# Seventh group's scores on strips, filler shared out, no single score ahead of strips

## The chip, the cores and the metric

The kernel runs on one core of a Trainium2 chip. The time is the device time of one execution in microseconds; the figure quoted is the median over runs. The engines are the PE (TensorE, matrix products), ScalarE (ACT), VectorE (DVE), GpSimd (POOL) and SP, which mainly issues DMA transfers.

## The reference

Two independent parts share one launch, and their outputs are put side by side.

```python
def _A_ref(x, wq, wk, wv, wo):          # x [1, 2048, 448], 16 heads of 28
    q = (x @ wq) as [heads, 2048, 28]
    k = x @ wk ; v = x @ wv             # one key/value head for all
    p = softmax(q @ k.T * 28 ** -0.5)
    return concat_heads(p @ v) @ wo

def _B_ref(x, w_r, w_i):                # x [1, 2048, 448]
    return irfft2(rfft2(x) * (w_r + 1j * w_i), s=(2048, 448))
```

All tensors are float32.

## The kernel before, in words

The kernel opens with the projections, the key tables and the first stage of the Fourier transform (the first 70 us or so). The rest, which the change concerns, is one long loop over the attention.

**Groups, chunks and steps.** The 2048 queries are cut into four chunks of 512, the 16 heads into four sets of four. A *group* is one chunk with one set, 16 groups in all, numbered 0 to 15 in the code; the text also says "seventh group" for number 6. A group has 16 *steps*, one for each 128 keys, so there are 256 steps. A step computes the scores of four heads against 128 keys (four products of 512 columns), ScalarE takes their exponentials out of the PSUM banks into `p`, and the PE multiplies them with the values (`values`, line 1218), summing a group's 16 steps in bank 7. The other seven banks serve scores and filler.

**Two ways to compute scores.** To keep float32 accuracy, keys and queries are split into a high and a low part, and a score is the sum of three products: high by high, high by low, low by high.

- A *stacked* step (`score`, line 1146) has the parts stacked over the 128 rows of the PE: `ka` holds the keys, `qa` the queries of a group. Each head's score is one product. `qa` is put together from `qh` and `ql` by nine DMAs of SP (lines 218, 219).
- A *strip* step (`strips`, line 1169) uses the PE as four strips of 32 rows, one for each head, at once. Each score takes three products, so a step has 12: four of high keys by high queries, four of high keys by low queries, four of low keys by high queries. It needs the keys repeated on all four strips. At the start these copies are in `kh` and `kl`. `STRIPS` (line 36) lists the groups that work on strips.

**Where the later strips' keys are kept.** `kh` and `kl` share their two buffers with the normed attention outputs, which are called `oh` (high part) and `ol` (low part), one pair for each chunk. From group 4 on those buffers belong to the outputs. So a later group on strips needs a fresh copy: `copy_keys` (line 787) writes the keys over the `oh` and `ol` of a chunk whose output projection is finished, in four DMAs of 512 KB from `ka` on SP's queue, two for `oh` (partitions 0 to 63 and 64 to 127) and two for `ol`. `KEYS` (line 38) says which copy each group takes. In the traces, products that read such a copy are named by `oh` and `ol`.

**What follows a group.** `group_out` copies bank 7 to `qraw`, and four rows of sums take a way through DRAM: out, back in another shape (`rs`), reciprocal on VectorE (`group_sums`, line 1038), out, and back spread over the partitions (`R`). `group_norm` (line 1049) multiplies and splits into `oh` and `ol`. When a chunk's four groups are normed, the chunk's four *output units* (`w_unit`) become ready. Each is the output projection of 128 rows: 11 products at line 1071, in pieces of 2, 3, 3 and 3. `wo_out` (line 1075) copies the result to `ya` and SP stores it. After the fourth unit of a chunk `copy_keys` follows.

**Filler.** Output units and the units of the last Fourier stage (`z_unit`, line 973, and `y_unit`, line 999) are *filler*: the PE does them between the scores of stacked steps. Strip steps take none. The middle of the Fourier part is VectorE's background work on the tile `X`, put between the other things that VectorE does; its result goes through DRAM (line 932) to the `z` units (loads at line 963).

**What sets the order.** Python code writes every engine's order out when the program is built. A loop keeps a clock for each engine (`clk`), a time at which each bank comes free (`free`), and a heap of events (`after`) with planned times; it decides step by step whether the PE takes scores, values or filler. `size` chooses how many steps' values are taken together (four where filler is at hand, else two), `share` how much filler a block may take. These planned times only decide the order; on the chip, the engines wait for each other through semaphores.

Of the kernel before, what the change touches and what calls it, by code (L numbers as in the profile page):

```python
# [32 lines left out]
LEAD = 7  # L33
WARM = 8, 8
FIRST = 8
STRIPS = 0, 1, 2, 3, 4, 7, 12, 15
HOME = {1: 0, 3: 1, 4: 0, 7: 1, 12: 0, 15: 1}
KEYS = {7: 0, 12: 1, 15: 2}
PLACES = (3, 5, 6, 8, 9, 10)


# [57 lines left out]
def kernel(ctx: ExitStack, tc: tile.TileContext, t: dict):  # L99
# [124 lines left out]
    with tc.tile_pool(name="f1", bufs=2) as f1[0], tc.tile_pool(name="w1", bufs=1) as w1, ExitStack() as ctx1:  # L224
# [305 lines left out]
        for c in range(1, NC):  # L530
            for g in range(NG):
                n = 4 * (c - 1) + g
# [152 lines left out]
    def after(when, dur, f, *a):  # L685
        heapq.heappush(events, (when, next(serial), dur, f, a))
# [339 lines left out]
    def group_out(c, g):  # L1026
        o = osb[c, g] = qraw[:, g, c * CW:c * CW + CW]
        V.tensor_copy(o, bank[7])  # L1028
        taken_out[0] += 1
        sd = dp.tile([4, CW], F32, name="sd", bufs=2)  # L1030
        rd = dp.tile([4, CW], F32, name="rd", bufs=2)
        rs = ap.tile([128, 16], F32, name="rs")
        nc.gpsimd.dma_start(sd, o[DH::32])  # L1033
        nc.gpsimd.dma_start(rs, sd.rearrange("i (a b) -> (i a) b", b=16))
        after(clk["dve"] + 10.0, 0.3, group_sums, c, g, rs, rd)

    def group_sums(c, g, rs, rd):
        V.reciprocal(rs, rs)
        nc.gpsimd.dma_start(rd.rearrange("i (a b) -> (i a) b", b=16), rs)
        for i in range(4):  # L1040
            nc.gpsimd.dma_start(R[32 * i:32 * i + DH], rd[i:i + 1].to_broadcast([DH, CW]))  # L1041
        after(clk["dve"] + 12.0, 2.1, group_norm, c, g)

    def group_norm(c, g):
        if g == 0:
# [227 lines left out]

    total = 12 * 2.22 + 16 * (0.88 + 0.73)

    def share(n):
        return max(1.8, n * (total - done[0]) / max(234 - done_steps, 3)) if n > 2 else 0.0

    done_steps, quota = 0, 0.0
    sc = 0  # L1280
    while done_steps < 256:
        k = sc // 4
        if 4 * k == sc and k // 16 in STRIPS and k < 256 and (done_steps >= k - 2 or not k):
            assert not waiting and KEYS.get(k // 16, -1) in spread_keys
            if k:
                vector(clk["pe"])
            strips(k)
            sc += 4
            if k < 2:
                first_fill(L + k)  # L1290
            while done_steps <= k - 2:
                values(done_steps, 1)
                done_steps += 1
                exps()
            n, since, gap, quota = size(), 0, 2, 0.0
            continue
# [3 lines left out]
        t_v = end[need - 1]  # L1300
        soon = min(free) <= clk["pe"] + 0.05
        more = sc < 4 * limit()
        if t_v <= clk["pe"] + 0.05 and (sc >= min(need + LEAD, 4 * limit()) or not soon):
            values(done_steps, n)
            done_steps += n
            exps()
            n = size()
            since, gap, quota = 0, 2, share(n)
        elif can_fill() and quota > 0 and since >= EARLY and gap >= 2 and (cur[0] or soon):
            t0 = done[0]  # L1310
            fill()
            quota -= done[0] - t0
            gap = 0
        elif more and soon:
            score(sc)
            sc += 1
            since += 1
            gap += 1
        elif sc == 1024 and can_fill():
            fill()  # L1320
        elif sc == 1024 and parts and normed[NC - 1] == NG - 1 and t_v > clk["pe"] + 0.5:
            partial()
        elif t_v <= min(free) or not more:
            values(done_steps, n)
            done_steps += n
            exps()
            n = size()
            since, gap, quota = 0, 2, share(n)
        else:
            score(sc)  # L1330
            sc += 1
            since += 1
            gap += 1
# [150 lines left out]
```

## Time and profile before

| | |
|---|---|
| median of 3 runs | 625.97 us (625.66 to 625.98) |
| profiled execution, span from first to last instruction | 624.6 us |
| what lies around the span (625.97 - 624.6) | 1.4 us |
| PE busy / ACT busy / DVE busy / POOL busy | 99% / 87% / 55% / 15% of the span |
| mean granted PE clock | 1.000 |
| DMA, mean over the span | 105 GB/s, 65.31 MB |

The busy times are shares of the whole span and so mix stages with different limits. A row of the timeline holds the start, the duration, the engine, the line, the tiles and the count of instructions merged into it; a bracket at its end tells how long the engine idled before it and who ended that. The records of the PE overlap, because its products are pipelined, so the pace is read from one row's start to the next row's start and not from durations. A row of the windows view gives, for a stretch of time, its length and then the busy time of PE, PEld, DVE, ACT and POOL with the count of instructions, the granted clock, the share of the 16 DMA engines and GB/s. The values of one step appear as eight records in the trace (each product runs in two passes) and as four rows in the program's order.

### The profile page before, as it was taken

The page shows a single profiled execution, that of the slowest core. Times are in us where ns is not written, and L with a number is a line of the kernel's source. Part 1 is how long each engine was busy: PE and PEld are TensorE (multiplying, and loading weights), DVE is VectorE, ACT ScalarE, POOL GpSimd, SP SyncE. Part 2 cuts the span into 40 slices and gives each one's busy share as a digit, 9 for nine tenths or more (in the row PEclk, how much of TensorE's full clock was granted, in tenths as well). Part 3 has the DMA queues.
Part 4 walks back from the last instruction along what each step waited for, and adds up shares of the span by engine and source line. Part 5 has one row for each costly group of instructions (what it writes and reads, how often), then busy time and mean ns, then how long its engine had stood idle before and what let it go on. Part 6 is the DMA issues. An engine that isn't in the chain of part 4 may idle for free.

```text
span 624.6 us, 13634 instructions
## 1 busy us (share of the span) xinstructions
PE 619.0 (99%) x5367; PEld 319.4 (51%) x5367; DVE 344.1 (55%) x685; ACT 541.0 (87%) x977; POOL 90.7 (15%) x168
## 2 busy tenths in 40 slices
PE   9999999999999999999999999999999999999997
PEld 7877633333333346654345565656653346564335
DVE  6999604979698987897732513227451231321014
ACT  4645799999999998889999888878889998888993
POOL 1021130102121101020321210030210101020200
PEclk9999999999999999999999999999999999999999
DMA  8856794001123331171664242294213131016001
GB/s 304 276 134 171 193 247 185 16 20 46 34 90 88 87 76 47 40 161 28 211 213 104 77 119 78 61 215 147 82 60 94 34 98 34 16 66 149 18 1 59
DMA packets 28748, 65.31 MB, mean 105 GB/s; under 512 B 6514, under 2 KB 15826, under 8 KB 27270
## 3 DMA queue, kind: packets, MB, share of 16 engines
q1 hardware_dynamic: 21066, 43.25, 24.9%
q0 software_dynamic: 7472, 20.96, 11.3%
q8 instruction: 42, 0.69, 0.5%
q10 hardware_dynamic: 144, 0.23, 0.1%
q14 instruction: 24, 0.19, 0.1%
HBM read 30.35 MB, written 16.30 MB: 75 GB/s over the span
## 4 chain that ended last, share of the span: by engine, by line
PE 98%; ACT 1%; DMA 1%; DVE 0%; issue 0%; DVEq 0%; ACTq 0%
PE banks L1218 39%; PE banks L1146 21%; PE banks L1169 18%; PE banks L330 7%; PE banks L1071 6%; PE banks L973 2%; PE banks L161 2%; PE banks L999 2%; PE banks L171 1%; DMA raw<-xw 1%; ACT p L1185 0%; PE banks L592 0%; DVE bs L188 0%; PE banks L502 0%; ACT al L615 0%
## 5 line engine op out<-in xcount | busy, mean ns | idle before, releaser
L1203 ACT ACTIVATE p<-banks 128x512 f32<-128x512 f32 x512 | 256.5, 702 | 39.4 <-PE banks L1218 18.3
L1218 PE MATMUL banks<-p,vs 128*32 128x512 f32 x2048 | 254.5, 600 | 0.2 <-DVE bs L188 0.2
L1185 ACT ACTIVATE p<-banks 128x512 f32<-128x512 f32 x262 | 145.5, 614 | 1.5 <-PE banks L1169 1.2
L1146 PE MATMUL banks<-qa,ka 128*128 128x512 f32 x512 | 145.7, 407 | 0.0
L1183 ACT ACTIVATE p<-banks 128x1024 f32<-128x1024 f32 x125 | 129.3, 1034 | 0.0
L1146 PEld LDWEIGHTS banks<-qa,ka 128*128 128x128 f32 x512 | 90.6, 188 | 53.3 <-ACT p L1203 34.5
L1218 PEld LDWEIGHTS banks<-p,vs 128*32 128x32 f32 x2048 | 49.3, 108 | 112.4 <-issue 108.7
L1028 DVE COPY qraw<-banks 128x512 f32<-128x512 f32 x15 | 10.4, 691 | 68.6 <-PE banks L1218 68.6
L1033 POOL DMA_DIRECT2D sd<-qraw x15 | 8.9, 596 | 244.1 <-DVE qraw L1028 244.1
L1075 DVE COPY ya<-banks 128x448 f32<-128x448 f32 x12 | 7.5, 624 | 52.2 <-PE banks L1071 36.4
L1041 POOL DMA_DIRECT2D R<-rd x60 | 30.4, 513 | 39.4 <-DMA rd<-rs 36.5
L1169 PE MATMUL banks<-qa,oh 32*128 32x512 f32 x384 | 35.6, 443 | 0.0
L1169 PE MATMUL banks<-qa,kh 32*128 32x512 f32 x384 | 35.5, 443 | 0.0
L856 DVE SCALAR_TENSOR_TENSOR X<-w,X 128x226 f32<-128x226 f32 (+2 forms) x72 | 34.1, 473 | 2.4
L1169 PEld LDWEIGHTS banks<-qa,kh 32*128 32x128 f32 x384 | 14.5, 183 | 40.3 <-ACT p L1185 40.3
L1169 PEld LDWEIGHTS banks<-qa,oh 32*128 32x128 f32 x384 | 14.6, 183 | 38.5 <-ACT p L1185 37.7
L981 DVE CAST zh<-banks 113x512 fp32r<-113x512 f32 (+1 forms) x16 | 11.0, 685 | 27.9 <-ACT p L1203 27.0
L1005 DVE COPY w<-banks 128x256 f32<-128x256 f32 x16 | 6.8, 423 | 35.0 <-PE banks L999 31.9
L334 ACT ACTIVATE qraw<-banks 128x512 f32<-128x512 f32 x16 | 9.4, 599 | 17.8 <-PE banks L330 17.7
L330 PE MATMUL banks<-xh,wqh 128*128 128x512 f32 x64 | 24.3, 412 | 0.2 <-DVE xh L278 0.2
L1071 PE MATMUL banks<-woh,oh 128*128 128x448 f32 x64 | 23.6, 369 | 0.0
L1071 PE MATMUL banks<-wol,oh 128*128 128x448 f32 x64 | 23.1, 362 | 0.0
(139 smaller groups left out, 754.6 us busy)
## 6 DMA issues: line engine op xcount, KB each, us to landing
xb<-xb SPq DMA_DIRECT2D x8, 512.0 KB
qa<-qa SPq DMA_DIRECT2D x8, 512.0 KB
ob<-yo SPq DMA_DIRECT2D x16, 256.0 KB
X<-t POOLq DMA_DIRECT2D x8, 452.0 KB, 15.5
wf<-w POOLq DMA_DIRECT2D x8, 452.0 KB, 3.9
c<-t POOLq DMA_DIRECT2D x8, 452.0 KB, 4.4
R<-rd POOLq DMA_DIRECT2D x60, 56.0 KB, 2.4
t<-bs SPq DMA_DIRECT2D x14, 226.0 KB
```

The lines of the kernel that those rows point to most:

```text
L161: mm(pa[r0:r0 + 32, e, 113 * k:113 * k + 113], f[:, 2 * r + k, 2 * p + e, h], cs1[:, 2 * r + k], start=True, stop=True)
L330: mm(pq[c, g], w[:, j, gs], x[:, j], start=(j == 0 and n == 0), stop=(j == 3 and n == 1))
L856: todo(226 * n, lambda d=d, q=q: STT(both(d), t[0].rearrange("p r n f -> p r (n f)"), q, both(a), op0=ALU.mult, op1=ALU.add))
L973: mm(pz[:w, j], fb["c2", q % 2][:, e, j, :w], fb["fi", q % 2][:, j], start=True, stop=True)
L1041: nc.gpsimd.dma_start(R[32 * i:32 * i + DH], rd[i:i + 1].to_broadcast([DH, CW]))
L1071: mm(p, x[c][:, g, s], w[:, m], start=(g == 0 and n == 0), stop=(g == NG - 1 and n == 2))
L1146: mm(bank[b], ka[:, kc * 128:(kc + 1) * 128], qa[c, g][:, h], start=True, stop=True)
L1169: mm(bank[bs[i]], k[r, kc * 128:(kc + 1) * 128], q[r], start=(n == 0), stop=(n == 2))
L1183: nc.scalar.activation(ends[1], banks[:, bs[1]:bs[1] + 2], AF.Exp, scale=SCALE)
L1185: nc.scalar.activation(pt[4 * st + i], bank[bs[i]], AF.Exp, scale=SCALE)
L1203: nc.scalar.activation(p, bank[b], AF.Exp, scale=SCALE)
L1218: mm(bank[7][32 * i:32 * i + 32], vs[:, kc], pt.pop(4 * st + i), start=(kc == 0), stop=(kc == 15))
```

## The change

Five things differ:

- Group 6 joins `STRIPS`; its keys are copy 0, the one that group 7 already uses.
- `group_sums` and `group_norm` are planned 3 us earlier each.
- `share` works toward two goals: by step 92 the first chunk's four output units are done (9.0 us of planned filler), by step 237 all filler. What is left is divided among the stacked steps alone.
- Filler pieces may stand one score apart (before: two) while much filler is left in a block.
- The last score of a stacked group is taken ahead of the values (`last`), so that it does not stand alone ahead of the strips.

```diff
-STRIPS = 0, 1, 2, 3, 4, 7, 12, 15
+STRIPS = 0, 1, 2, 3, 4, 6, 7, 12, 15
-KEYS = {7: 0, 12: 1, 15: 2}
+KEYS = {6: 0, 7: 0, 12: 1, 15: 2}
...
-        after(clk["dve"] + 10.0, 0.3, group_sums, c, g, rs, rd)
+        after(clk["dve"] + 7.0, 0.3, group_sums, c, g, rs, rd)
...
-        after(clk["dve"] + 12.0, 2.1, group_norm, c, g)
+        after(clk["dve"] + 9.0, 2.1, group_norm, c, g)
...
+    goals = (92, 9.0), (237, total)
+
     def share(n):
-        return max(1.8, n * (total - done[0]) / max(234 - done_steps, 3)) if n > 2 else 0.0
+        until, goal = next((x for x in goals if x[0] > done_steps + 2), goals[-1])
+        left = sum(st // 16 not in STRIPS for st in range(done_steps, until))
+        return n * (goal - done[0]) / max(left, 3) if n > 2 else 0.0
...
         if 4 * k == sc and k // 16 in STRIPS and k < 256 and (done_steps >= k - 2 or not k):
-            assert not waiting and KEYS.get(k // 16, -1) in spread_keys
             if k:
                 vector(clk["pe"])
+            assert not waiting and KEYS.get(k // 16, -1) in spread_keys
             strips(k)
...
         more = sc < 4 * limit()
-        if t_v <= clk["pe"] + 0.05 and (sc >= min(need + LEAD, 4 * limit()) or not soon):
+        last = more and sc == 4 * limit() - 1 and min(free) <= clk["pe"] + 0.35
+        if t_v <= clk["pe"] + 0.05 and (sc >= min(need + LEAD, 4 * limit()) or not soon) and not last:
             values(done_steps, n)
...
-        elif can_fill() and quota > 0 and since >= EARLY and gap >= 2 and (cur[0] or soon):
+        elif can_fill() and quota > 0 and since >= EARLY and gap >= (2 if quota < 2.3 else 1) and (cur[0] or soon):
...
-        elif more and soon:
+        elif more and (soon or last):
             score(sc)
```

The order of the instructions shows where this lands. The PE, where the kernel before goes from the stacked steps of group 6 to the strips of group 7 (values at `p,vs`, stacked scores at `qa,ka`, strip products at `qa,oh` and `qa,ol`; the brackets name the semaphores that a row waits for, those with DMAHW being landings of SP's transfers):

```order
L1146 MATMUL banks<-qa_1057,ka 128x512 [waits Activation_49] x8
L1218 MATMUL banks<-p,vs 32x512 x8
L1146 MATMUL banks<-qa_1057,ka 128x512 [waits Activation_49]
L1169 MATMUL banks<-qa_1058,oh 128x512 [waits DMAHW2_49,Activation_49]
L1169 MATMUL banks<-qa_1058,oh 128x512
L1169 MATMUL banks<-qa_1058,oh 128x512 [waits DMAHW3_49,Activation_49]
L1169 MATMUL banks<-qa_1058,oh 128x512 [waits Activation_49]
L1169 MATMUL banks<-qa_1058,oh 128x512 x4
L1169 MATMUL banks<-qa_1058,ol 128x512 [waits DMAHW4_49]
L1169 MATMUL banks<-qa_1058,ol 128x512
L1169 MATMUL banks<-qa_1058,ol 128x512 [waits DMAHW5_49]
```

Ahead of the strips stands a single score, and between it and the block with the first chunk's last output unit five pairs of stacked steps. The PE in the changed kernel, at its first product on a copied key, now in group 6:

```order
L1071 MATMUL banks<-woh,ol 128x448
L1146 MATMUL banks<-qa_1058,ka 128x512 [waits Activation_49] x5
L1218 MATMUL banks<-p,vs 32x512 x16
L1169 MATMUL banks<-qh,oh 128x512 [waits DMAHW1_49,DVE_49]
L1169 MATMUL banks<-qh,oh 128x512 [waits Activation_49]
L1169 MATMUL banks<-qh,oh 128x512 [waits DMAHW2_49,Activation_49]
L1169 MATMUL banks<-qh,oh 128x512 [waits Activation_49]
L1169 MATMUL banks<-ql,oh 128x512 x4
L1169 MATMUL banks<-qh,ol 128x512 [waits DMAHW3_49]
L1169 MATMUL banks<-qh,ol 128x512
L1169 MATMUL banks<-qh,ol 128x512 [waits DMAHW4_49]
L1169 MATMUL banks<-qh,ol 128x512
```

The single score is gone, and between the last product of the first chunk's output units (`woh,ol`) and the first strip product stand five scores and the values of four steps. SP's queue, as the difference between the two kernels, around the copy that these strips read:

```order
-L218 DMA qa_1057<-qh 32x512
-L218 DMA qa_1057<-ql 32x512
-L219 DMA qa_1057<-qa_1057 64x2048
 L1077 DMA oa<-ya 128x448 x2
 L1057 DMA lows<-ol 128x512
```

The nine transfers that build the stacked queries of group 6 are gone; the copy itself (line 793, four transfers) stands in the same place behind the fourth store of `ya`.

## The prediction

> **What bounds the kernel now.** I read the page's chain of waits first, then the timeline of the PE in the stretches that the change rewrites, then the DMA queue.
>
> ```profile
> PE 98%; ACT 1%; DMA 1%; DVE 0%; issue 0%; DVEq 0%; ACTq 0%
> ```
>
> The chain that ends last runs on the PE for 98% of the span, so a microsecond counts if it is put into the PE's order or taken out of it. Three kinds of steps share that order. A stacked pair without filler, around 280 us:
>
> ```profile
> 275.73 2.14 PE L1146 MATMUL banks<-qa,ka 128*128 128x512 f32 x8
> 277.80 1.93 PE L1218 MATMUL banks<-p,vs 128*32 128x512 f32 x16
> 279.65 2.11 PE L1146 MATMUL banks<-qa,ka 128*128 128x512 f32 x8
> 281.69 1.92 PE L1218 MATMUL banks<-p,vs 128*32 128x512 f32 x16
> 283.54 2.14 PE L1146 MATMUL banks<-qa,ka 128*128 128x512 f32 x8
> ```
>
> The first column is the start. Two steps (eight scores, then the values of two steps) take 279.65 - 275.73 = 3.92 us, the next pair 3.89, and no row carries a bracket for an idle PE. A strip step, and how strips are entered:
>
> ```profile
> 291.37 0.50 PE L1146 MATMUL banks<-qa,ka 128*128 128x512 f32 x1
> 291.80 0.74 PE L1169 MATMUL banks<-qa,oh 32*128 32x512 f32 x8
> 292.36 0.41 PE L1169 MATMUL banks<-qa,ol 32*128 32x512 f32 x4
> ...
> 296.50 1.06 PE L1218 MATMUL banks<-p,vs 128*32 128x512 f32 x8
> ...
> 298.40 1.06 PE L1218 MATMUL banks<-p,vs 128*32 128x512 f32 x8
> ```
>
> One strip step takes 298.40 - 296.50 = 1.90 us. The single score ahead of the strips takes 0.43 us (291.37 to 291.80). Within a strip step the third product, the only one that reads the low keys `ol`, starts 0.56 us after the first. Last, a block of four stacked steps with a whole output unit as filler:
>
> ```profile
> 261.97 1.66 PE L1146 MATMUL banks<-qa,ka 128*128 128x512 f32 x6
> 263.47 0.36 PE L1071 MATMUL banks<-woh,oh 128*128 128x448 f32 x1
> ...
> 266.83 0.36 PE L1071 MATMUL banks<-woh,ol 128*128 128x448 f32 x1
> 267.03 1.08 PE L1146 MATMUL banks<-qa,ka 128*128 128x512 f32 x4
> 268.04 3.64 PE L1218 MATMUL banks<-p,vs 128*32 128x512 f32 x32
> 271.61 2.34 PE L1146 MATMUL banks<-qa,ka 128*128 128x512 f32 x9
> ```
>
> This is the last output unit of the first chunk. Its last product starts at 266.83. Call T = 267.03 the start of the score behind it. Then come 1.01 us for four scores (so 0.25 for one), and 3.57 us for the values of four steps.
>
> **The change part by part.** *The seventh group on strips.* By the order, the stacked pairs fall from 17 to 9, the blocks of four stay at 23, and 16 steps become strip steps. Eight pairs of about 3.905 us leave (31.24), 16 strips of 1.90 come (30.40): -0.84. The eight `qa` copies and the big ninth one for this group leave SP's queue; nothing on the PE waited for them.
>
> *No lone head.* Three entries into strips lose their single score, which then stands in a block: 0.43 - 0.23 = 0.20 each, -0.60 together. I take 0.23 from the pair (1.85 us of scores and a little over 0.2 of switching make 2.07).
>
> *Filler shared out.* The number of filler products stays the same and the PE is the bound with and without them, so moving them costs and gains nothing: 0. One place bounds a gain:
>
> ```profile
> 510.22 2.04 PE L1146 MATMUL banks<-qa,ka 128*128 128x512 f32 x6
> 512.10 1.03 PE L973 MATMUL banks<-fi,c 128*113 128x128 f32 x8
> ```
>
> Six scores between two filler pieces last 1.88 us where the six at 261.97 last 1.50. That stall may go (-0.4) or come up elsewhere (+0.4). I keep 0, as most fillers show none.
>
> *Sums and norms placed earlier.* The vector engine may now stand longer at a landing.
>
> ```profile
> L1049 DVE TENSOR_TENSOR qraw<-qraw,R 128x512 f32<-128x512 f32 x15 | 10.3, 685 | 13.7 <-DMA R<-rd 13.7
> L1038 DVE RECIPROCAL rs<-rs 128x16 f32<-128x16 f32 x15 | 3.7, 247 | 10.2 <-DMA rs<-sd 10.1
> ```
>
> It waits 24 us in 30 such places already, with no term of it on the chain. Up to 3 us more each would have to push a bank's eviction or the first filter outputs, which are loaded well ahead of the PE:
>
> ```profile
> 320.38 0.71 POOL L963 DMA_DIRECT2D c<-t  x1
> ...
> 335.28 1.03 PE L973 MATMUL banks<-fi,c 128*113 128x128 f32 x8
> ```
>
> The load is issued 15 us before its product. I take 0, between 0 and +2 if that cover is used up.
>
> *The keys for the seventh group.* This is the term that decides. `KEYS` gives group 6 the copy 0 of the keys, which overwrites `oh` and `ol` of the first chunk. So it cannot start before the first chunk's last output unit has read them, and strips of group 6 cannot start before it has landed. Before, this copy served group 7:
>
> ```profile
> 267.94 0.33 SPq L1077 DMA_DIRECT2D oa<-ya  x1
> 268.31 1.13 SPq L793 DMA_DIRECT2D oh<-ka  x2
> 269.55 4.49 SPq L793 DMA_DIRECT2D ol<-ka  x2
> ```
>
> ```profile
> 268.00:269.00 1.00, 1.00 (x13) 0.37 (x16) 1.00 (x4) 0.49 (x2) 0.00 (x0) 1.00 0.21 81
> ...
> 278.00:279.00 1.00, 1.00 (x12) 0.26 (x8) 0.97 (x4) 1.00 (x4) 0.52 (x1) 1.00 0.89 197
> 279.00:280.00 1.00, 1.00 (x10) 0.31 (x3) 1.00 (x5) 1.00 (x4) 1.00 (x3) 1.00 0.26 90
> ```
>
> The last two columns are the DMA engines' share and GB/s. The four copies of 512 KB are issued from T + 1.28 on, and the transfers keep the engines full until 279.6 or so, T + 12.6: together with the 224 KB of `ya` some 2.3 MB at about 200 GB/s. Strips of group 7 came at 291.80, 12 us later, so nobody waited.
>
> After the change the last unit sits in the last stacked block before the strips. Behind T stand only five scores and four steps of values: 1.01 + 0.23 + 3.57 = 4.81 us. The first strip product is reached at T + 4.81, its third at T + 5.37. The high keys arrive half by half and end about midway through the copy, the second half of the low keys at T + 12.6. The wait is 12.6 - 5.4 = **7.2 us**, cut in pieces by the products whose half has landed. Behind it on the PE's queue stands everything; ScalarE has no scores to exponentiate, the vector engine's copy of the sixth group's output waits for values behind the strips, and its filter work waits behind that copy, late by the same time as the PE that will use it. No work is placed in the gap. Afterwards a strip step costs 1.90 as before, so nothing is made up.
>
> Bounds of the wait: the two other copies are the nearest rows.
>
> ```profile
> 406.80 1.66 SPq L793 DMA_DIRECT2D oh<-ka  x2
> ...
> 420.00:422.00 2.00, 2.00 (x13) 1.55 (x10) 0.00 (x0) 1.61 (x4) 0.00 (x0) 1.00 0.96 239
> ...
> 562.68 1.13 SPq L793 DMA_DIRECT2D oh<-ka  x2
> ...
> 572.00:574.00 2.00, 2.00 (x18) 0.44 (x17) 0.00 (x0) 2.00 (x5) 0.00 (x0) 1.00 0.72 160
> ```
>
> The third took until about 573.5, 10.8 us from its issue, which makes the wait 6.7; the second ran into other loads and lasted about 14 us, which makes it 9.9. Nothing else large is due at this place (the store of the filter work starts some 40 us later), so I take 7.2.
>
> The sum: -0.84 - 0.60 + 7.2 = +5.8 us. The profiled span of 624.6 becomes 630.4; the runs' median lies 1.37 above the span (625.97), so **631.7 us**.
>
> [...]
>
> **The rivals.**
>
> *A: the PE's clock falls as well.* Inside the program the PE has not stood still for microseconds; at its two ends it has:
>
> ```profile
> 1.07 3.59 PE L253 MATMUL banks<-idle 128*128 128x256 bf16 x16 [1.07 <-DVE warm L248]
> ...
> 5.16 1.77 PE L330 MATMUL banks<-xh,wqh 128*128 128x512 f32 x4 [0.17 <-DVE xh L278]
> 6.76 0.62 PE L330 MATMUL banks<-xl,wqh 128*128 128x512 f32 x2
> ```
>
> ```profile
> 620.39 0.37 PE L1071 MATMUL banks<-woh,ol 128*128 128x448 f32 x1
> ...
> 624.00:624.60 0.60, 0.00 (x0) 0.00 (x0) 0.00 (x0) 0.00 (x0) 0.00 (x0) 0.73 0.00 0
> ```
>
> At the start four products of 512 columns take 6.76 - 5.16 = 1.60 us, later ones 0.23 each: the PE ran slow until about 6.5, 5.4 us after its first product. At the end the granted clock of the last 0.6 us averages 0.73, so it halved at about 624.3, 3.5 us after the last product. For this rival: the wait of 7.2 us is twice that. Against: it is cut by products at the landings, into pieces of under 3 us each (the high keys' two halves, then the low keys' two, some 2.5 us apart), and the rows do not show whether such short bursts keep the clock up. Price: half speed for up to 5.4 us loses up to 2.7 us: 631.7 + 2.7 = 634.4. [...] Chance 0.25.
>
> *B: the copy lands later still*, because another transfer shares the engines or `ya` reaches SP late: the second copy's 14 us, wait 9.9 in place of 7.2: 634.4. For it: one of three copies was so. Against: at 406 filter loads ran beside it, which at 256 to 269 are not due yet. Chance 0.10.
>
> *C: faster.* The copy lands before the strips ask for it, and 1.44 us are won: 624.5. It needs the low keys by T + 5.4, so 2.3 MB in the 4.1 us behind the issue: 560 GB/s. The stretch with the most traffic had 410:
>
> ```profile
> 10.00:12.00 2.00, 2.00 (x11) 1.65 (x10) 1.71 (x3) 1.01 (x3) 0.00 (x0) 1.00 1.03 410
> ```
>
> So it would need a first strip that asks for less than the whole copy; but the first strip step reads all four partition groups of both key tiles. Chance 0.05. *D: in between,* the copy runs near that 410 GB/s: 5.7 us, landing at T + 7.0, wait 1.6, total +0.2: 626.1, no change. Chance 0.05.
>
> **How the numbers follow.** Forecast 0.55, A 0.25, B 0.10, C 0.05, D 0.05. The forecast's own range, from a wait of 6.7 with the stall at 510 gone (-0.4) to one of 7.5 with 0.7 of delays on the vector engine, is 630.8 to 632.7. The range for 8 in 10 takes in A and B to a little over their 634.4 and leaves out C and D: 630.5 to 635.5. A measurement of this kernel tells some 0.2% (1.25 us) from no change: faster is C (0.05), the same is D with a remainder below it (0.04), slower is the rest (0.91).
>
> **What would show it.** Right: one stretch in the changed kernel, between the sixth group's last stacked block and its first strip values, in which the PE's products of the high and low keys (`oh`, `ol`) stand singly with idle brackets that name the copy, 6.5 to 8 us in all; the copy's issue 1.3 us behind the last output product of the first chunk; strip steps at 1.90 us before and after; stacked blocks at 9.6 to 11 us by the number of their filler products; the three entries into strips directly behind the values; no wait at the entries of groups 12 and 15, where 19 us and more lie between the last output unit and the strips. A is right if the first strips behind the gap take more than 1.90 each and the granted clock of that stretch is under 1. Wrong: no gap at that place (then C, and the time is near 624.5), or a gap and yet a time under 630, which would mean that the shared filler won something that I priced at 0. A second gap, at the first filter products of the ninth group, would mean that the vector engine's earlier waits did cost.

## The result, and the profile after

The changed kernel takes 635.76 us (median, 635.23 to 636.11), the kernel before 625.93 on the same chip: a ratio of 1.0158, 95% interval 1.0143 to 1.0172, so about 9.8 us slower. The forecast was 631.7 with a range up to 635.5: the sign and the place were right, the size was not, and rival A (the clock) came true, though its own 634.4 was 1.4 us short as well.

The profiled execution has a span of 634.0 us against 624.6, so 9.4 more. First the view of the windows, three stages of the loop in the kernel before and then in the changed one: from the first stacked block behind group 4's strips to the block with the ninth group's first filter products, from there to the end of group 12's strips, and from there to the end of the loop.

```profile
221.67:333.79 112.12, 112.12 (x824) 54.31 (x820) 79.77 (x179) 105.50 (x201) 16.97 (x30) 1.00 0.40 113
333.79:504.34 170.55, 170.55 (x1256) 95.95 (x1252) 64.08 (x122) 147.41 (x284) 25.16 (x45) 1.00 0.35 95
504.34:608.70 104.36, 104.36 (x787) 53.09 (x783) 20.95 (x39) 94.51 (x177) 11.19 (x21) 1.00 0.22 57
```

```profile
220.85:342.90 122.05, 115.88 (x952) 50.81 (x948) 80.42 (x181) 104.65 (x187) 17.50 (x31) 0.96 0.33 95
342.90:512.97 170.07, 170.07 (x1250) 95.25 (x1246) 63.20 (x118) 147.19 (x282) 24.60 (x44) 1.00 0.34 94
512.97:618.04 105.07, 105.07 (x792) 53.77 (x788) 22.20 (x42) 94.58 (x177) 11.19 (x21) 1.00 0.21 57
```

All of the loss is in the first stage: 122.05 - 112.12 = +9.93. The second stage has -0.48, the third +0.71. Only the first stage of the changed kernel has an idle PE (122.05 - 115.88 = 6.17 us) and a clock under 1. What comes ahead of these stages is 0.82 shorter, which has nothing to do with the change: in this execution the first four products at line 330 took 1.01 us, where they took 1.60 in the kernel before, and the lead of 0.8 is there before 70 us.

The PE's timeline of the changed kernel at the sixth group's end, the place that the prediction named:

```profile
254.84 0.36 PE L1071 MATMUL banks<-woh,ol 128*128 128x448 f32 x1
255.04 1.53 PE L1146 MATMUL banks<-qa,ka 128*128 128x512 f32 x5
256.51 3.64 PE L1218 MATMUL banks<-p,vs 128*32 128x512 f32 x32
261.06 0.50 PE L1169 MATMUL banks<-qh,oh 32*128 32x512 f32 x2 [0.92 <-DMA oh<-ka]
263.76 0.49 PE L1169 MATMUL banks<-qh,oh 32*128 32x512 f32 x2 [2.20 <-DMA oh<-ka]
263.77 0.81 PE L1169 MATMUL banks<-ql,oh 32*128 32x512 f32 x4
266.13 0.80 PE L1169 MATMUL banks<-qh,ol 32*128 32x512 f32 x2 [1.55 <-DMA ol<-ka]
268.43 0.79 PE L1169 MATMUL banks<-qh,ol 32*128 32x512 f32 x2 [1.50 <-DMA ol<-ka]
269.15 1.94 PE L1218 MATMUL banks<-p,vs 128*32 128x512 f32 x8
271.01 0.80 PE L1169 MATMUL banks<-qh,oh 32*128 32x512 f32 x4
...
274.46 0.51 PE L1169 MATMUL banks<-qh,oh 32*128 32x512 f32 x4
```

T, the start of the score behind the last output product, is 255.04. Without a wait the strips would begin 3.57 us behind the values, at 260.08, and their third product at 260.64. The four brackets are the landings of the four halves of the keys; the last lands at 268.43 = T + 13.39, so the **wait is 268.43 - 260.64 = 7.8 us**. Two strip steps later, at 274.46, the PE should have been at 260.08 + 2 x 1.90 = 263.88. It lost 10.58 in all, so **2.8 us besides the wait**, and the values of one step, which take 1.07 at full speed, take 1.94. The view of the windows of that stretch:

```profile
260.00:262.00 2.00, 0.65 (x6) 0.21 (x2) 1.97 (x5) 0.71 (x2) 0.00 (x0) 1.00 0.95 197
262.00:264.00 2.00, 0.23 (x4) 0.27 (x6) 1.81 (x5) 0.00 (x0) 0.00 (x0) 1.00 0.98 229
264.00:266.00 2.00, 0.58 (x6) 0.06 (x2) 0.31 (x1) 0.00 (x0) 0.00 (x0) 0.57 1.01 221
266.00:268.00 2.00, 0.80 (x2) 0.29 (x2) 0.00 (x0) 0.99 (x2) 0.00 (x0) 0.50 0.57 139
...
272.00:274.00 2.00, 2.00 (x16) 0.20 (x8) 0.00 (x0) 1.25 (x3) 0.00 (x0) 0.50 0.00 0
274.00:276.00 2.00, 2.00 (x24) 0.65 (x20) 1.40 (x3) 1.28 (x3) 0.42 (x1) 0.87 0.00 0
```

The granted clock is 0.5 from (1.00 - 0.57) x 2 / 0.5 = 1.72 us ahead of 266.00 to (1.00 - 0.87) x 2 / 0.5 = 0.52 us behind 274.00: 264.28 to 274.52, 10.24 us. It fell while the wait still lasted and stayed low for 6 us after the last key had landed. Of the four executions on record two have a mean granted clock of 0.991, as the profiled one, and two 0.995, and these two were no faster (636.11 and 635.68 us against 635.84 and 635.23); how their loss divides into wait and clock no trace tells. The DMA engines are full at some 200 to 230 GB/s until 267. SP's queue in the changed kernel, to be read beside its rows at 268 in the kernel before:

```profile
246.81 9.47 SPq L1077 DMA_DIRECT2D oa<-ya  x2
256.39 1.19 SPq L793 DMA_DIRECT2D oh<-ka  x2
257.67 4.47 SPq L793 DMA_DIRECT2D ol<-ka  x2
```

The copy is issued at T + 1.35 (before: T + 1.28).

### The profile page after: what moved, and what is told of

Its sections match the earlier page's. It is cut to its first block, busy times and chain, and to the rows that moved or that the text cites. A ratio compares the mean times of both kernels' runs of the same rounds, so it can differ in the third digit from the quotient of the medians.

```text
span 634.0 us, 13892 instructions
## 1 busy us (share of the span) xinstructions
PE 622.3 (98%) x5495; PEld 315.3 (50%) x5495; DVE 344.7 (54%) x685; ACT 540.0 (85%) x963; POOL 90.7 (14%) x168
## 4 chain that ended last, share of the span: by engine, by line
PE 97%; DMA 1%; ACT 1%; SPq 0%; DVE 0%; issue 0%; DVEq 0%; ACTq 0%
PE banks L1218 38%; PE banks L1169 20%; PE banks L1146 18%; PE banks L330 7%; PE banks L1071 6%; PE banks L973 2%; PE banks L161 2%; PE banks L999 2%; DMA ol<-ka 1%; PE banks L171 1%; PE banks L253 1%; ACT p L1185 0%; SPq L793 0%; PE banks L592 0%; DVE bs L188 0%
## 5 line engine op out<-in xcount | busy, mean ns | idle before, releaser
L1218 PE MATMUL banks<-p,vs 128*32 128x512 f32 x2048 | 257.9, 604 | 0.2 <-DVE bs L188 0.2
L1203 ACT ACTIVATE p<-banks 128x512 f32<-128x512 f32 x448 | 224.5, 666 | 39.3 <-PE banks L1218 21.0
L1185 ACT ACTIVATE p<-banks 128x512 f32<-128x512 f32 x298 | 165.1, 614 | 12.8 <-PE banks L1169 6.4
L1183 ACT ACTIVATE p<-banks 128x1024 f32<-128x1024 f32 x139 | 143.8, 1035 | 0.0
L1146 PE MATMUL banks<-qa,ka 128*128 128x512 f32 x448 | 129.0, 407 | 0.0
L1146 PEld LDWEIGHTS banks<-qa,ka 128*128 128x128 f32 x448 | 79.0, 188 | 43.0 <-ACT p L1203 26.7
L1049 DVE TENSOR_TENSOR qraw<-qraw,R 128x512 f32<-128x512 f32 x15 | 10.3, 688 | 27.0 <-DMA R<-rd 26.9
```

Of the source, the lines that this page charges most:

```text
L1146: mm(bank[b], ka[:, kc * 128:(kc + 1) * 128], qa[c, g][:, h], start=True, stop=True)
L1183: nc.scalar.activation(ends[1], banks[:, bs[1]:bs[1] + 2], AF.Exp, scale=SCALE)
L1185: nc.scalar.activation(pt[4 * st + i], bank[bs[i]], AF.Exp, scale=SCALE)
L1203: nc.scalar.activation(p, bank[b], AF.Exp, scale=SCALE)
L1218: mm(bank[7][32 * i:32 * i + 32], vs[:, kc], pt.pop(4 * st + i), start=(kc == 0), stop=(kc == 15))
```

## The experiments

"Lost in the gap" below is worked out as above: the third strip step's start, less the place where it would be without a wait.

**1. The group taken off strips again.** Everything else of the change stays; the first goal becomes 10.0 so that the copy comes in time for group 7.

```diff
-STRIPS = 0, 1, 2, 3, 4, 6, 7, 12, 15
-KEYS = {6: 0, 7: 0, 12: 1, 15: 2}
+STRIPS = 0, 1, 2, 3, 4, 7, 12, 15
+KEYS = {7: 0, 12: 1, 15: 2}
...
-    goals = (92, 9.0), (237, total)
+    goals = (92, 10.0), (237, total)
```

> The change without its first part: the seventh group stays on stacked scores (the first goal of the filler is raised from 9.0 to 10.0, so that the first chunk's last piece still fits ahead of the copy). Theory (the wait for the copied keys and the slow clock behind it are the whole loss of 10 us): no wait anywhere, granted clock 1.00 throughout, and the time of the kernel before less what the three lone scores cost (0.6) plus what single blocks lose to ScalarE (up to 1): 625.3 to 626.5. Rival (the spread filler, the earlier sums and norms or the kept-back last score carry part of the loss): 628 or more.

Measured 627.25, ratio 1.0022 (1.0013 to 1.0032), mean granted clock 0.999: between the two ranges. The copied keys cost the main part, but the rest of the change (here with the first goal at 10.0), for which the prediction has a gain of 0.6, costs 1.2 to 1.4 (by the medians and by the ratio). Experiments 5 and 6 follow this.

**2. The gap filled.** The wait stays, but the PE works through it: 33 products without use ahead of group 6's first strip.

```diff
     def strips(st):
...
+        if st == 96:
+            for _ in range(33):
+                mm(bank[bs[0]], ka[:, :128], ka[:, 512:1024], start=True, stop=True)
```

> The changed kernel with 33 extra products of 512 columns ahead of the first strip product of the seventh group, about 7.6 us of work at 0.23 each, into a bank that the strips then overwrite; the PE is busy while the copy lands. Theory (the clock is a cost of its own, 2.8 us by the strips behind the gap, and it falls because the PE stands nearly still): the copy lands as before, the clock stays at 1.00 and the time falls by 2.5 to 3.0, to about 633. Rival (the slow stretch is only another sign of the wait, or products do not hold the clock): 635.5 to 636.

Measured 633.48, ratio 1.0118 (1.0101 to 1.0135). The PE's timeline, with the dummies and the one wait that is left:

```profile
255.74 1.53 PE L1146 MATMUL banks<-qa,ka 128*128 128x512 f32 x5
257.20 3.64 PE L1221 MATMUL banks<-p,vs 128*32 128x512 f32 x32
260.78 7.78 PE L1168 MATMUL banks<-ka 128*128 128x512 f32 x33
268.49 0.50 PE L1172 MATMUL banks<-qh,oh 32*128 32x512 f32 x4
...
270.01 0.50 PE L1172 MATMUL banks<-qh,ol 32*128 32x512 f32 x2 [0.56 <-DMA ol<-ka]
```

The copy landed at T + 14.27, 0.9 later than in the changed kernel, and still the first stage, now 221.54 to 341.77, is 122.05 - 120.23 = 1.8 us shorter; the mean granted clock is 0.999 in place of 0.991. So the clock's fall is a cost of its own, set by the idle PE and not by the copy, and 1.8 + 0.9 = 2.7 agrees with the 2.8 worked out above. By the medians of four runs each the kernel is 2.3 us faster.

**3. The output units earlier.** All four stand in the first two stacked blocks of the sixth group's stretch, and the copy starts 6 us sooner.

```diff
-    goals = (92, 9.0), (237, total)
+    goals = (89, 9.0), (237, total)
```

> The changed kernel with the first goal at step 89 in place of 92: the first chunk's four output units stand in two blocks instead of three, so that 12.2 us of other work lie between the last unit and the first strip. Theory (only the distance to the copy's landing counts, some 12.6 to 13 us behind the last unit): a wait of under 0.5 us at the third strip product, clock 1.00, time 625.3 to 626.5. Rival (strips in the seventh group cost something beside the wait, or the copy moves back with the units' denser filler): 628 or more.

Measured 626.35, ratio 1.0007 (0.9996 to 1.0018). SP's queue and the PE at the first strip:

```profile
250.09 1.19 SPq L793 DMA_DIRECT2D oh<-ka  x2
```

```profile
260.89 0.51 PE L1169 MATMUL banks<-qh,oh 32*128 32x512 f32 x4
261.22 0.40 PE L1169 MATMUL banks<-ql,oh 32*128 32x512 f32 x4
261.45 0.39 PE L1169 MATMUL banks<-qh,ol 32*128 32x512 f32 x2
262.03 0.50 PE L1169 MATMUL banks<-qh,ol 32*128 32x512 f32 x2 [0.18 <-DMA ol<-ka]
```

One wait of 0.18 is left and the clock stays up (mean 0.999), with the same strips, the same copy and the same source. For the gap, only the distance between the last output unit and the first strip counts. No gain over the kernel before remains, though: the three stages differ from its by +0.12, -0.66 and +0.71 us, so the third loses what the second wins (experiments 5 and 6).

**4. What sets the copy's rate.** The prediction took 200 GB/s from the rows without knowing what makes it. Three variants: the keys written to DRAM early and read from there onto 64 partitions at a time; the same, onto all 128 at once; and the two halves from `ka` on two queues.

```diff
+    kd = dp.tile([2, 64, S], F32, name="kd")     # filled early from kh and kl
...
-                nc.sync.dma_start(d[64 * u:64 * u + 64].bitcast(F32), ka[64 * k:64 * k + 64].bitcast(F32))
+                nc.sync.dma_start(d[64 * u:64 * u + 64].bitcast(F32), kd[k])
```

> The changed kernel with the keys written to DRAM once, early (2 transfers of 512 KB behind the first key tables), and every later copy read from there instead of from the stacked keys in SBUF. Theory (the copy is slow because both its ends lie in SBUF: 200 GB/s in each of the four copies traced, where loads from DRAM ran at up to 410): the copy is through some 6 us after its issue, the wait shrinks to 2 to 3 us, the clock stays at 1.00, time 626.5 to 628. Rival (SP's queue or the size of the pieces sets 200 GB/s): the copy takes 10 to 11 us as before, 635 to 636.

```diff
+    kd = dp.tile([2, 128, S], F32, name="kd")
...
-            for u in range(2):
-                nc.sync.dma_start(d[64 * u:64 * u + 64].bitcast(F32), ka[64 * k:64 * k + 64].bitcast(F32))
+            nc.sync.dma_start(d.bitcast(F32), kd[k])
```

> The changed kernel, with the keys of all heads written to DRAM early (two of 1 MB) and each copied key tile read from there by one transfer of 1 MB onto all 128 partitions, where the change sends two transfers of 0.5 MB onto 64 partitions each. Theory: a transfer onto 64 partitions reaches half of what one onto 128 does, and that sets the 180 to 229 GB/s in the stage of the copy. Then the two copies land some 5 us sooner after their issue, the third product waits 2 to 3 us in place of 7.8, the clock stays nearly full and the time is 626.5 to 628.5. Rival: what sets the rate is something else (the queue, the size of its packets): the copies take the same 10 us, the wait stays at 7 to 8 us, the clock falls and the time is 635 to 637.

```diff
-                nc.sync.dma_start(d[64 * u:64 * u + 64].bitcast(F32), ka[64 * k:64 * k + 64].bitcast(F32))
+                (nc.gpsimd if u else nc.sync).dma_start(d[64 * u:64 * u + 64].bitcast(F32), ka[64 * k:64 * k + 64].bitcast(F32))
```

> The changed kernel with the two halves of each copied key tile issued from two queues, SyncE's and GpSimd's, so that both can run at once; the source stays SBUF. Theory that one queue works off its transfers one after another and each alone runs at about 200 GB/s: the copies land 4 to 5 us sooner, the wait is 2 to 4 us, the time 626.5 to 629. Rival, that the sixteen DMA engines or the ports of SBUF set the rate whichever queue issues: the copies take the same 10 us, the time is 635 to 637.

Measured: 637.07 (ratio 1.0179, 1.0162 to 1.0196) from DRAM in halves, 631.41 (1.0080, 1.0064 to 1.0095) from DRAM onto all partitions, 634.21 (1.0123, 1.0107 to 1.0138) on two queues. None of the three lies in a range that was named. The last landings in the PE's timeline, first in halves from DRAM, then onto all partitions, then on two queues:

```profile
266.38 0.79 PE L1174 MATMUL banks<-qh,ol 32*128 32x512 f32 x2 [1.07 <-DMA ol<-kd]
268.67 0.79 PE L1174 MATMUL banks<-qh,ol 32*128 32x512 f32 x2 [1.50 <-DMA ol<-kd]
```

```profile
257.52 3.64 PE L1222 MATMUL banks<-p,vs 128*32 128x512 f32 x32
263.39 0.50 PE L1173 MATMUL banks<-qh,oh 32*128 32x512 f32 x4 [2.23 <-DMA oh<-kd]
265.74 0.50 PE L1173 MATMUL banks<-qh,ol 32*128 32x512 f32 x4 [1.62 <-DMA ol<-kd]
...
270.60 0.50 PE L1173 MATMUL banks<-qh,oh 32*128 32x512 f32 x4
```

```profile
266.80 0.92 PE L1169 MATMUL banks<-qh,oh 32*128 32x512 f32 x4 [5.69 <-DMA oh<-ka]
```

In halves, the last 512 KB land 2.3 us behind those ahead of them, whether from DRAM (268.67 - 266.38 = 2.29) or from SBUF (268.43 - 266.13 = 2.30): 228 GB/s. Onto all partitions, the second 1 MB lands 265.74 - 263.39 = 2.35 us behind the first: 446 GB/s. The fullest window of 2 us has 229 GB/s in both runs in halves, and 418 in the one onto all partitions. The source made no difference; the number of partitions written did, by a factor of two. The transfer onto all partitions was also twice as large, but the size does not set the rate: at the start of the kernel before four transfers of 512 KB onto all 128 partitions (`raw`, line 267) stand on the queue with only 40 KB beside them, and the DMA engines moved 410 GB/s between 4.00 and 6.00 us. The last low key now lands 9.7 us behind T (256.06 there), not 13.4, and 5.7 us are lost in the gap (270.60 less 257.52 + 3.57 + 3.80), not 10.6. My expectation of 626.5 to 628.5 still missed: the first of the two transfers took 6.0 us from its issue (257.40) to its landing, and the clock fell to half for 3.4 us (the last section shows it). On two queues all four halves are there 10.8 us behind T, with one wait of 5.69 us ahead of them, so two queues overlap a part, with at most 311 GB/s in a window of 2 us.

Why a transfer onto 64 partitions goes at half the rate, none of these runs shows.

**5. The small parts one by one,** each put alone into the kernel before: the last score kept back (no lone heads); the shared filler; the earlier sums and norms.

```diff
-        if t_v <= clk["pe"] + 0.05 and (sc >= min(need + LEAD, 4 * limit()) or not soon):
+        last = more and sc == 4 * limit() - 1 and min(free) <= clk["pe"] + 0.35
+        if t_v <= clk["pe"] + 0.05 and (sc >= min(need + LEAD, 4 * limit()) or not soon) and not last:
...
-        elif more and soon:
+        elif more and (soon or last):
```

> The kernel before with one part of the change alone: the last score before a strips step is kept back until two or more stand together (no lone head). By the prediction's term this is worth -0.60 us (three lone scores of 0.20): 625.4. By what the two traces and the run with group 6 stacked showed since: the score that is kept back arrives in a longer run of scores, and these runs wait for ScalarE to free a bank (nine scores in a row cost 2.97 in place of 2.33); then the gain is eaten up and the kernel takes 626.0 to 627.2.

```diff
+    goals = (92, 10.0), (237, total)
+
     def share(n):
-        return max(1.8, n * (total - done[0]) / max(234 - done_steps, 3)) if n > 2 else 0.0
+        until, goal = next((x for x in goals if x[0] > done_steps + 2), goals[-1])
+        left = sum(st // 16 not in STRIPS for st in range(done_steps, until))
+        return n * (goal - done[0]) / max(left, 3) if n > 2 else 0.0
...
-        elif can_fill() and quota > 0 and since >= EARLY and gap >= 2 and (cur[0] or soon):
+        elif can_fill() and quota > 0 and since >= EARLY and gap >= (2 if quota < 2.3 else 1) and (cur[0] or soon):
```

> The kernel before with the shared filler alone (the new share and the shorter gap), first goal 10.0 so that its keys of group 7 come as early as before. By the prediction's term (0, bounds -0.4 and +0.4) it takes 625.6 to 626.4. By what the run with group 6 stacked showed (+1.2 with share, early sums and no lone heads together, and no lone heads alone within 0.6 of nothing) the share costs it: 627.0 to 627.7, in waits of scores for banks that ScalarE frees.

```diff
-        after(clk["dve"] + 10.0, 0.3, group_sums, c, g, rs, rd)
+        after(clk["dve"] + 7.0, 0.3, group_sums, c, g, rs, rd)
...
-        after(clk["dve"] + 12.0, 2.1, group_norm, c, g)
+        after(clk["dve"] + 9.0, 2.1, group_norm, c, g)
```

> The kernel before with the earlier sums and norms alone (7.0 and 9.0 in place of 10.0 and 12.0 in the planner). By the prediction's term (0, bound +2) it takes 625.6 to 626.4: the planner's units come one stacked pair earlier, and their number stays. Rival: this is where the run with group 6 stacked lost its 1.2, by units that fall into blocks with too little between their scores: 627.0 or more.

| alone in the kernel before | median us | ratio, 95% interval | first stage | second | third |
|---|---|---|---|---|---|
| no lone heads | 625.80 | 0.9993 (0.9984 to 1.0002) | +0.02 | +0.09 | -0.25 |
| shared filler | 627.56 | 1.0024 (1.0015 to 1.0033) | +0.63 | -0.37 | +1.32 |
| earlier sums and norms | 626.40 | 1.0006 (0.9997 to 1.0015) | -0.09 | -0.19 | +0.27 |
| group 6 stacked (experiment 1) | 627.25 | 1.0022 (1.0013 to 1.0032) | +0.54 | -0.51 | +0.80 |

The last columns are the length of the three stages less that of the kernel before, from one trace each. Only the shared filler can be told from nothing, and it costs 1.5 us, as its second expectation had it; the earlier sums and norms lie in their first range, and the 625.80 without lone heads lies between its two expectations. Of the filler's loss 0.63 stands in the first stage. There the old rule put the four output units into four blocks of four steps and the new one, in this run, into two blocks, each with two units, and four more pairs. Each block begins with a change from values to scores; a block of four with a unit takes 271.61 - 261.97 = 9.64 us, less eleven products at 0.20 that is 7.4, where two pairs take 7.8. Two blocks given up at some 0.4 us each come near the 0.63; this is an estimate from these rows, and it was not tried alone. The larger part is in the third stage, and experiment 6 looks for it.

**6. Does ScalarE hold the scores up?** In the run with group 6 stacked the last block of group 14 ends in nine scores:

```profile
572.66 2.99 PE L1146 MATMUL banks<-qa,ka 128*128 128x512 f32 x9
575.58 3.64 PE L1218 MATMUL banks<-p,vs 128*32 128x512 f32 x32
```

```profile
573.18 0.30 PEld L1146 LDWEIGHTS banks<-qa,ka 128*128 128x128 f32 x2 [0.30 <-ACT p L1203]
573.67 0.19 PEld L1146 LDWEIGHTS banks<-qa,ka 128*128 128x128 f32 x1 [0.19 <-ACT p L1203]
```

```profile
565.68 9.90 ACT L1203 ACTIVATE p<-banks 128x512 f32<-128x512 f32 x20 [0.88 <-PE banks L1146]
```

They take 575.58 - 572.66 = 2.92 us, where nine scores at 271.61 in the kernel before took 2.26. The weight loads (second view) wait for exponentials, and ScalarE (third view) works through 20 of them without a break, one in 0.49 us: it has fallen behind, the banks are full, and the scores wait for it. To test that, the exponentials of the stacked steps from step 184 on were halved, in the run with group 6 stacked, in the kernel before, and in the run with the shared filler alone. In a first try VectorE wrote the other half:

```diff
-            nc.scalar.activation(p, bank[b], AF.Exp, scale=SCALE)
+            w = 256 if i >= 4 * 184 else CW
+            nc.scalar.activation(p[:, :w], bank[b][:, :w], AF.Exp, scale=SCALE)
+            if w < CW:
+                V.memset(p[:, w:], 1.0)        # the later three: nc.gpsimd.memset
```

> The run with group 6 stacked (627.25), with the exponentials of the stacked steps from step 184 on over the first half of the columns alone (VectorE writes 1.0 in the other half): what is left out is half of these weights. Only ScalarE's time per exponential changes there. Theory that the waits of 0.37 and 0.72 us in the runs of scores at the ends of the blocks are ScalarE's, which has no idle time there: they go, and the nine scores at 572.66 take 2.33 in place of 2.99; the time is 625.8 to 626.3. Rival, that TensorE itself is slow there (operands, order of the products): the nine scores still take 2.9 and the time stays at 627.2.

> The run with group 6 stacked, with the exponentials of the stacked steps from step 184 on over half the columns, and GpSimd writing 1.0 in the other half (half of these weights are left out). Theory that ScalarE sets the pace of the runs of scores there: the nine scores that took 2.99 us take 2.3, the waits of 1.4 us from step 184 to the end of the loop go, and the time is 625.6 to 626.4. Rival, TensorE's own order or operands: nothing moves, 627.2.

> The kernel before with the same halving from step 184 on (half of these weights are left out). It had one such wait, 0.57 us in the run of six scores at 510.22; by the theory that ScalarE sets it, it goes and the time is 625.4 to 626.0; by the rival nothing moves.

> The kernel before with the shared filler alone (627.56) and the same halving (half of these weights are left out). By the theory the 1.1 us of waits from step 184 on go and what is left is the 0.7 us of two more blocks around step 80: 626.3 to 626.8. By the rival it stays at 627.5.

The first try took 626.78, between its two expectations, and told nothing: the nine scores now stood 0.62 us for VectorE, which was late with a filter unit's banks because of the writes put on it.

```profile
573.77 0.96 PE L1146 MATMUL banks<-qa,ka 128*128 128x512 f32 x3 [0.62 <-DVE w L1007]
```

With the writes on GpSimd the nine scores take 574.36 - 572.00 = 2.36:

```profile
572.00 2.43 PE L1146 MATMUL banks<-qa,ka 128*128 128x512 f32 x9
574.36 3.64 PE L1221 MATMUL banks<-p,vs 128*32 128x512 f32 x32
```

| | median us (whole and halved on different chips) | third stage, whole | third stage, halved |
|---|---|---|---|
| group 6 stacked | 627.25, halved 626.11 | 105.16 | 104.17 |
| kernel before | 625.93, halved 625.78 (the same chip) | 104.36 | 104.21 |
| shared filler alone | 627.56, halved 626.55 | 105.68 | 104.59 |

Halved, the shared filler's loss in the third stage falls from 105.68 - 104.36 = 1.32 to 104.59 - 104.21 = 0.38, that of group 6 stacked from 0.80 to nothing, and the first stage, where nothing was halved, keeps its +0.63. So 1.32 - 0.38 = 0.94 us of the shared filler's loss there are scores that wait for ScalarE: filler that is taken out of a block leaves a longer run of scores at its end, and such a run waits for exponentials of 0.49 us each; the nine scores took 2.92 us, 0.32 a score, where a score without the wait takes 0.23 to 0.25. What makes the 0.38 that is left stays open. The two medians with the shared filler lie in the ranges of this theory; that of the kernel before, 0.15 lower, cannot be told from no change. There the first five of the six scores at 510 no longer wait for ScalarE, but the sixth waits 0.16 for a bank that VectorE frees, so the six take 1.81 us in place of 1.88.

**7. Looking for a version that beats both.** The units earlier as in experiment 3, once with the lone heads back (the first goal at 89 as there), once with the old share from step 87 on:

```diff
-        last = more and sc == 4 * limit() - 1 and min(free) <= clk["pe"] + 0.35
+        last = False
```

> The changed kernel with the output units of the first chunk spread over the last two stacked blocks ahead of the copy (as in the run with the units earlier, 626.35) and without keeping the last score back: lone heads come back. By the prediction's -0.60 for lone heads this costs 0.6 us: 626.9. By the theory that keeping the score back makes ScalarE late, it gains 0.7 to 1.4 us: 625.0 to 625.7, under the kernel before.

```diff
-    goals = (92, 9.0), (237, total)
-
     def share(n):
-        until, goal = next((x for x in goals if x[0] > done_steps + 2), goals[-1])
-        left = sum(st // 16 not in STRIPS for st in range(done_steps, until))
-        return n * (goal - done[0]) / max(left, 3) if n > 2 else 0.0
+        if done_steps < 87:
+            left = sum(st // 16 not in STRIPS for st in range(done_steps, 89))
+            return n * (9.0 - done[0]) / max(left, 3) if n > 2 else 0.0
+        return max(1.8, n * (total - done[0]) / max(234 - done_steps, 3)) if n > 2 else 0.0
```

> The run with the units earlier once more, with the old share from step 87 on (every block of four gets at least 1.8 us of filler). If the shared filler is what takes away the gain of group 6 on strips, the stage from step 184 on no longer has the runs of nine scores that wait for ScalarE, and the kernel takes 625.0 to 625.7. If it is ScalarE in sum, whose work is the same however the filler lies, the waits only stand elsewhere and the time is 626.0 to 626.6.

Measured 626.84 (ratio 1.0009, 1.0000 to 1.0018) and 626.50 (1.0005, 0.9996 to 1.0014). Neither beats the kernel before, so neither of the gains that were hoped for came. The first lies at the 626.9 of the prediction's term, but its ratio is within 0.0002 of experiment 3's, so it tells nothing of the lone heads. The second lies in the range of ScalarE in sum. With the old share the third stage is at 104.38 again, as the theory of the share has it, but the second stage has +0.48. The one idle time of the PE there is not ScalarE's:

```profile
421.79 0.69 DVE L1049 TENSOR_TENSOR qraw<-qraw,R 128x512 f32<-128x512 f32 x1 [5.53 <-DMA R<-rd]
...
424.85 1.86 PE L1146 MATMUL banks<-qa,ka 128*128 128x512 f32 x6 [0.47 <-DVE w L1007]
```

VectorE stood 5.53 us for a landing ahead of a norm and came late to the banks of the filter units behind it (`w`), and six scores waited 0.47 for it. The other run has 0.26 at the same place. In the kernel before, the norm stands behind those filter outputs at this place (423.81 us) and waits for nothing. So the earlier norms can cost, in orders other than the changed kernel's; whether the later norms would win the 0.48 back was not tried.

## Why the prediction was wrong in size

- **The place and the mechanism were right.** One gap, at the seventh group's first strips, cut into four by the landings of the four halves; issue 1.35 us behind T (said: 1.28); no wait at groups 12 and 15; no second gap at the ninth group's filter products; strip steps at 1.90 again from 274.46 us on. The four idle brackets add up to 6.17 us, a little under the 6.5 to 8 that was named as the sign.
- **The wait** was put at 7.2 and was 7.8. Failed was the landing, T + 12.6, taken from another place in the program; here it was T + 13.4. The bounds (6.7 to 9.9) held it.
- **The clock** is the step that failed: it stood outside the sum, as a rival with 0.25, because the wait is cut into pieces of under 3 us. In the trace those pieces do not help. In the 3.41 us (a third of the 10.24) ahead of the fall, 260.87 to 264.28, two brackets of 0.20 (what is left of the 0.92) and 2.20 leave the PE about 1 us of work, and the clock fell. Its price, put at up to 2.7, was 2.8, but that they agree is luck: 2.7 came from 5.4 us at half speed, and there were 10.24, of which only the 6.1 behind the last landing could cost. Nor do the traces hold to the 5.4: the granted clock reads 1.00 in that stretch of the kernel before, and in the changed kernel the same first four products took 1.01 us, 0.25 each, from 4.90 us on, 3.8 us behind the PE's first. Forecast plus these two corrections: 631.7 + 0.6 + 2.8 = 635.1. In the profiled span the account closes: 630.4 + 0.6 + 2.8, and 1.0 more since of the gains of 1.44 only 0.65 - 0.23 = 0.42 came, less the 0.8 of the start, is 634.0.
- **Group 6 on strips, -0.84,** was not tried alone. The first stage, +9.93 with 10.58 lost in the gap, leaves -0.65, but this holds a lone head and the shared filler too. Experiment 3's first stage less its wait of 0.18 is 0.60 shorter than experiment 1's, which keeps group 6 stacked and has another first goal; both figures have the sign and about the size.
- **No lone head, -0.60,** is not settled: alone it has a ratio of 0.9993, an interval from -1.0 to +0.1 us that holds both -0.60 and nothing. Its trace speaks for less, since its stages add up to -0.14; the kept-back score then stands in a longer run of scores, and such runs can be ScalarE's (experiment 6), but no run here tells that for these entries.
- **The shared filler, 0 (-0.4 to +0.4),** is the second failed step: +1.5 alone. I had argued that the PE is the bound with and without it, and that the stall at 510 is one place that may go. That stall was the sign of the second limit: ScalarE is busy for 94.51 of the third stage's 104.36 us, and a block whose filler is taken away waits for it, 0.94 of the 1.32 lost in that stage (for the stall at 510 itself this is shown only in part, by the run of experiment 6). In the changed kernel the last two stages have -0.48 and +0.71, together +0.23, where -0.40 was due from two lone heads.
- **Sums and norms, 0,** held: +0.4 by the median, with an interval from -0.2 to +0.9 us that contains zero. VectorE's own waits grew, and in the changed kernel the PE never stood for VectorE in the three stages (its idle 6.17 us are all the copy's); two runs of experiment 7 show where it can. The row of the page's groups in the changed kernel, whose last columns are the idle time and its cause:

```profile
L1049 DVE TENSOR_TENSOR qraw<-qraw,R 128x512 f32<-128x512 f32 x15 | 10.3, 688 | 27.0 <-DMA R<-rd 26.9
```

It was 13.7 before, and the earlier sums and norms alone make it 26.7.

## What to carry to other kernels

When a buffer is reused for a copy, count the time from its last reader to the first reader of the copy against the whole landing (13.4 us here), and place the last reader that much earlier: the same change with its copy 6 us sooner lost nothing that can be told. The wait of 7.8 us on the PE cost 10.6: price the clock as part of the wait, even when single products cut it into pieces. And before filler is counted as free to move, look at the second busiest engine: here ScalarE was busy for 91% of the third stage, and filler between the scores was what let it catch up: the shared filler lost 1.32 us there, and 0.38 with the exponentials halved.

## What the runs showed of the hardware

- **Short bursts did not keep the clock up.** The clock was granted at 0.5 for 10.24 us in the changed kernel, 6.8 us in the run on two queues (whose wait of 5.69 was not cut) and 3.4 us in the one onto all partitions (brackets of 2.23 and 1.62). The last of these in the view of the windows:

```profile
266.00:268.00 2.00, 2.00 (x16) 0.39 (x16) 0.00 (x0) 1.68 (x4) 0.00 (x0) 0.63 0.04 8
268.00:270.00 2.00, 2.00 (x16) 0.82 (x20) 0.00 (x0) 0.87 (x2) 0.00 (x0) 0.52 0.00 0
```

  (2.00 x 0.37 + 2.00 x 0.48) / 0.5 = 3.4 us at half speed. After the wait it did not come back with the first products: from 267.69 to 271.10 in the changed kernel, the second third of its 10.24 us, the PE was idle only for the last 0.74 us of the bracket ahead of 268.43, and the clock stayed at 0.5 to 274.52. The three lengths are near three, two and one times 3.41 us, a third of the 10.24; what sets them, no run shows.
- **The number of partitions that a transfer writes set its rate:** 228 GB/s onto 64, from DRAM as from SBUF, and 446 onto 128, from DRAM, in the same place of the same program.
